# Another hand-written order of steps for a local-attention and SwiGLU kernel on one core

## The chip, the cores and the metric

The kernel runs on one core of a Trainium2 chip. The metric is the device time of one execution in microseconds (us); of several runs the median is given. Engines are named as in the profile: PE (matmuls; PEld its weight loads), DVE, ACT, POOL, and SP, which computes nothing and issues DMAs. "banks" is the accumulator memory that PE writes: eight banks of 128 x 512 float32.

## The reference

Two parts follow each other. First an attention for 4 batches, 8 heads, 768 positions and head size 64, with a bias that falls linearly with distance; a position sees the last 96 positions and the first 8 ("global") keys. Then, on the 4 x 768 = 3072 tokens of 8 x 64 = 512 numbers, a SwiGLU layer with 1536 hidden units. Cut to what matters:

```python
keep = (pos_k < 8) | ((rel >= 0) & (rel < 96))            # rel = query - key
scores = q @ k.T / sqrt(64) - slope[h] * dist              # dist: rel, or 96 for far globals
a = softmax(where(keep, scores, -1e9))
x = (a @ v).transpose(0, 2, 1, 3).reshape(3072, 512)
g, val = x @ w_gate, x @ w_val                             # 512 -> 1536
out = (g * sigmoid(g) * val) @ w_out                       # 1536 -> 512
```

Inputs and output are float32; on the chip the matmuls take float16.

## The kernel before, in words

**Tiling.** A batch has two halves of 384 positions. Batch b and half h make tile t = 2b + h of 384 tokens; eight tiles pass through the second part. The heads of a batch are taken in four pairs (0 to 3), two pairs to a head group.

**What sets the order.** Nothing is scheduled by a program: the string `ORDER` (L67 to L147) lists steps, the last loop of the kernel runs them in this order, and each step records its instructions. Each engine executes its own instructions in that order, one behind the other, and waits at an instruction whose inputs or whose destination are not ready; everything behind it on the same engine waits too. DMAs are issued by the engine that the step names and queue there in the same way: SP issues transposes and output transfers, POOL nearly all loads (L292, L333, L344, L351, L356).

```python
for step in ORDER.split():
    name, *args = step.split(".")
    WORK[name](*(int(a) if a.isdigit() else a for a in args))
```

**Banks.** `single` and `double` deal one or two of the eight banks to a step while the steps are recorded, and `release` puts them back at the end of a list. So the order of the steps also decides which earlier step a matmul must wait for before it may overwrite a bank. In the same way buffers go round: two for output rows (`osb`), two for V (`vS`), two each for the staged rows of keys (`kst`) and queries (`qst`), two for transposed keys (`kN`), four for transposed queries (`qT`).

**The steps that matter here**, with the lines that record them:

- Warm-up: `fill.n` is n matmuls on ones (L394), ahead of the first real work; `fill.23` stands at the end of the order before.
- Batch 0: `Lh` loads half of the keys or queries, `T` transposes them on PE (L417), `cast` changes types (L400) on ACT (`.A`) or DVE (`.V`).
- Batch 1: its first two pairs come by two big loads (`L4`, L333), its other rows by one load per head (`Lr`, L344: a row load; `Lr.b.i.h` has i = 0 for keys and 1 for queries). Batches 2 and 3 come by row loads alone.
- `D.b.p.i` transposes the rows of head pair p (i = 0 keys, 1 queries) by a DMA on SP's queue (L483); `K` copies the keys into place (L490).
- `Z.b.P` is the clearing: POOL writes zeros into two corners of batch b's V buffer (L309), which it may do when the batch that had the buffer before is done with it. `Lv.b.c` then loads chunk c of V, seven chunks per batch (L292). `G` copies the global rows of V on SP (L303). `X` makes the crossed copy of V (L319), which needs all its chunks.
- Attention: `c` scores (L520), `x` exponentials on ACT (L530), `m` masks on DVE, `w` sums for the softmax (L630, L597), `W` weighs V (the L614 matmuls, one block per batch, half and head group), `i`, `j`, `r` (L659, L663) turn the sums into reciprocals and put them in place, `p` scales (L678).
- Second part: `g.t.f` and `v.t.f` are the products of gates and values (L693, four matmuls each: a product step), f being one of twelve blocks of hidden units; `ga` and `gb` (or `va` and `vb`) are its two halves of two matmuls. `t` is a tanh on ACT (L699), `s` and `h` are the rest of the activation on DVE (L703, L709).
- `o.t.i.part` is a fourth of an output row block (L734, three matmuls: an output part; L723 in the last rows), `e.t.i` the output copy of the finished block on ACT into an `osb` buffer (L752) and its transfer by SP (L753; L747 and L748 in the last rows).

While the products of one tile run, the loads, transposes and scores of the next batch are under way; the order mixes their steps by hand.

Of the kernel before, what the change touches and what calls it, by code (L numbers as in the profile page):

```python
# [809 lines left out]
```

## Time and profile before

| | |
|---|---|
| time before | 238.52 us, median of 3 runs (237.11 to 238.77) |
| the profiled execution | 237.59 us |
| its span, first to last instruction | 235.8 us |
| moved by DMA | 25.97 MB, mean 110 GB/s |
| granted clock of PE, mean | 1.000 |

Rows of the views read so. In a group, "PE banks L693 x116" is engine, destination, line and count, with the busy time and the stretch ahead of it. A row of the order in time gives start, duration (or the sum of a run of equal instructions), engine, line, operation, destination<-sources, shape, and in brackets how long the engine stood before it and for what. A row of a window gives start:end, its length, then PE, PEld, DVE, ACT, POOL and SP busy (with counts), the granted clock, the busy share of the DMA engines and GB/s. A row of a waits view gives the waiting instruction, what released it, and the time, count and longest. "SPq" and "POOL ... DMA_DIRECT2D" rows are the issue of a DMA, not its transfer; "DMA to landing" is the time from issue until the data are there.

### The profile page before, as it was taken

The numbers are of one execution on the slowest core, as the hardware profiler recorded it, in microseconds if no ns is written. First come the engines' busy times: TensorE is split into PE (matmuls) and PEld (weight loads), VectorE is DVE, ScalarE is ACT, GpSimd is POOL, SyncE is SP. The second block draws the span as 40 slices with busy tenths as digits, with TensorE's granted clock in tenths as the row PEclk, the third lists the DMA queues.
The fourth block names the chain that finished last, engine by engine and source line by source line (L and its number), as shares of the span: only waits on it lengthen the run. The fifth ranks groups of instructions, "written<-read, shape, count | busy, mean of one in ns | idle before, by whom it ended". The sixth has DMA issues, their size and how long they took to land.

```text
span 235.8 us, 6107 instructions
## 1 busy us (share of the span) xinstructions
PE 229.6 (97%) x2515; PEld 133.6 (57%) x2515; DVE 169.5 (72%) x389; ACT 116.3 (49%) x219; POOL 79.8 (34%) x113
## 2 busy tenths in 40 slices
PE   7999899998999999999999999999999999999998
PEld 4466566554455666655556556565555565555446
DVE  3998898869466789969979998984495876542200
ACT  3688847546842734357858674440424341311321
POOL 8976759731581599788100000000000000000000
DMA  6999999999999899999996311010012000010332
GB/s 171 194 180 188 204 197 178 171 140 122 188 145 184 190 161 135 124 153 153 143 204 152 39 49 47 0 47 0 3 44 89 0 3 0 1 44 3 135 129 93
DMA packets 88324, 25.97 MB, mean 110 GB/s; under 512 B 78048, under 2 KB 85256, under 8 KB 88296
## 3 DMA queue, kind: packets, MB, share of 16 engines
q0 software_dynamic: 67120, 14.25, 79.2%
q1 hardware_dynamic: 20488, 10.74, 23.4%
q10 hardware_dynamic: 688, 0.59, 0.7%
q8 instruction: 19, 0.31, 0.6%
q14 instruction: 9, 0.07, 0.1%
HBM read 28.93 MB, written 6.29 MB: 149 GB/s over the span
## 4 chain that ended last, share of the span: by engine, by line
PE 66%; DMA 23%; POOL 7%; ACT 3%; issue 1%; POOLq 0%; ACTq 0%
PE banks L693 39%; PE banks L734 20%; DMA kst<-in_k_dram 9%; DMA wo<-in_moe_w_out_dram 8%; DMA wv<-in_moe_w_val_dram 4%; DMA out_dram<-osb 2%; POOL vS L292 2%; PE banks L520 2%; PE banks L614 2%; PE banks L723 1%; PE banks L394 1%; POOL k L284 1%; POOL q L284 1%; POOL wg L351 1%; PE banks L630 1%
## 5 line engine op out<-in xcount | busy, mean ns | idle before, releaser
L699 ACT ACTIVATE th<-banks 128x384 f32<-128x384 f32 x96 | 44.3, 494 | 59.4 <-PE banks L693 56.4
L693 PE MATMUL banks<-xT,wv 128*128 128x384 f16 x384 | 71.4, 326 | 0.0
L693 PE MATMUL banks<-xT,wg 128*128 128x384 f16 x384 | 71.2, 326 | 0.1
L709 DVE TENSOR_TENSOR hT<-banks,sl 128x384 f16<-128x384 f32 x96 | 50.8, 552 | 21.2 <-PE banks L693 19.8
L734 PE MATMUL banks<-wo,hT 128*128 128x512 f16 x276 | 65.8, 379 | 0.0
L703 DVE SCALAR_TENSOR_TENSOR sl<-th,banks 128x384 f32<-128x384 f32 x96 | 50.1, 547 | 17.3 <-ACT th L699 16.7
L693 PEld LDWEIGHTS <-wv 128*128 128x128 f16 x384 | 37.3, 98 | 26.3
L693 PEld LDWEIGHTS <-wg 128*128 128x128 f16 x384 | 36.7, 98 | 25.6 <-issue 0.6
L734 PEld LDWEIGHTS <-hT 128*128 128x128 f16 x276 | 26.3, 98 | 28.2 <-issue 0.2
L530 ACT ACTIVATE at<-banks 128x976 f16<-128x976 f32 (+3 forms) x28 | 25.5, 958 | 12.1 <-PE banks L520 12.1
L292 POOL DMA_DIRECT2D vS<-in_v_dram x28 | 25.2, 908 | 9.8 <-DMA vS<-in_v_dram 6.7
L752 ACT ACTIVATE osb<-banks 128x512 f32<-128x512 f32 x23 | 13.5, 599 | 23.3 <-PE banks L734 14.6
L344 POOL DMA_DIRECT2D qst<-in_q_dram x20 | 17.2, 860 | 8.8 <-DMA wo<-in_moe_w_out_dram 4.1
L539 DVE TENSOR_TENSOR at<-at,masks 128x976 f16<-128x976 f16 (+3 forms) x26 | 15.7, 643 | 4.1 <-ACT at L530 4.1
L663 DVE STREAM_TRANSPOSE rb<-dR 128x384 f32<-128x384 f32 x32 | 16.7, 553 | 2.8 <-ACT dR L659 2.7
L344 POOL DMA_DIRECT2D kst<-in_k_dram x20 | 16.7, 841 | 2.6 <-DMA vS<-in_v_dram 1.1
L520 PE MATMUL banks<-qT,kT 64*64 64x152 f16 (+9 forms) x456 | 9.2, 214 | 1.6 <-DMA qT<-qst 1.6
L520 PEld LDWEIGHTS <-kT 64*64 64x64 f16 x456 | 7.2, 107 | 5.8 <-issue 4.8
L678 DVE TENSOR_TENSOR xT<-banks,rb 128x384 f16<-128x384 f32 x16 | 8.4, 546 | 1.3 <-PE banks L614 1.2
L319 ACT COPY vX<-vS 64x1792 f16<-64x1792 f16 (+2 forms) x6 | 7.3, 1220 | 3.3 <-DMA kst<-in_k_dram 3.2
L637 ACT COPY ns<-banks 128x768 f32<-128x768 f32 x6 | 4.7, 807 | 7.9 <-PE banks L614 7.9
L614 PEld LDWEIGHTS <-vS 64*64 64x64 f16 x228 | 6.6, 107 | 2.6 <-issue 2.1
(77 smaller groups left out, 165.2 us busy)
## 6 DMA issues: line engine op xcount, KB each, us to landing
out_dram<-osb SPq DMA_DIRECT2D x23, 256.0 KB, 2.1
vS<-in_v_dram POOLq DMA_DIRECT2D x24, 120.0 KB, 7.7
qst<-in_q_dram POOLq DMA_DIRECT2D x20, 96.0 KB, 7.2
kst<-in_k_dram POOLq DMA_DIRECT2D x20, 96.0 KB, 6.7
wg<-in_moe_w_gate_dram POOLq DMA_DIRECT2D x6, 256.0 KB, 7.3
wv<-in_moe_w_val_dram POOLq DMA_DIRECT2D x6, 256.0 KB, 8.2
wo<-in_moe_w_out_dram POOLq DMA_DIRECT2D x3, 512.0 KB, 18.2
k<-in_k_dram POOLq DMA_DIRECT2D x3, 192.0 KB, 5.7
```

The source lines that it names most:

```text
L292: nc.gpsimd.dma_start(out=v_of(b)[r0:r0 + n, c, heads(g), :], in_=v[b, heads(g), KC * c:KC * c + n, :].rearrange("h p d -> p h d"))
L344: nc.gpsimd.dma_start(out=rows_of(i, b, h // 2)[:, :, h % 2, :], in_=KQ[i][b, h].rearrange("(t p) d -> p t d", p=128))
L520: nc.tensor.matmul(sc[64 * r:64 * r + 64, hi, col:col + n], lhsT=kTs[2 * g + r][d, k0:k0 + 64], rhs=qTs[b, 2 * g + r][d, q0:q0 + n], start ...
L530: nc.scalar.activation(out=at[:, :, 0:w], in_=sc[:, :, 0:w], func=AF.Exp, scale=scale)
L539: ENG[e].tensor_mul(a2, a2, masks[:, 2 * g:2 * g + 2, x:x + w])
L663: nc.vector.transpose(rb.rearrange("p (n i) -> p n i", i=32), rbs[b, half][:, g, r].unsqueeze(2).broadcast_to([128, TB // 32, 32]))
L693: nc.tensor.matmul(gv[t, f, which][:, 0:TB], lhsT=w[:, c, 128 * f:128 * f + 128], rhs=xTs[t][:, c, :], start=(c == 0), stop=(c == NC - 1))
L699: nc.scalar.activation(out=th, in_=gv[t, f, 0][:, 0:TB], func=AF.Tanh, scale=0.5)
L703: nc.vector.scalar_tensor_tensor(out=sl, in0=gv[t, f, "t"], scalar=1.0, in1=gv[t, f, 0][:, 0:TB], op0=AluOp.add, op1=AluOp.mult)
L709: nc.vector.tensor_mul(hTs[t][:, f, :], gv[t, f, 1][:, 0:TB], gv[t, f, "s"])
L734: nc.tensor.matmul(ops_t[t, i], lhsT=hTs[t][:, f, 128 * i:128 * i + 128], rhs=wo[:, f, :], start=(f == 0), stop=(f == NFF - 1))
L752: nc.scalar.mul(out=osb, in_=ops, mul=0.5)
```

## The change

Only the string `ORDER` is changed. Every step but these stays as it was and stands elsewhere: `fill.11 fill.5` (16 warm-up matmuls) become `fill.24`, and `fill.23` at the end is dropped; `g.0.1`, `v.0.8`, `v.0.9` and `v.0.10` are split into their halves; three casts, some copies of transposed keys and queries, crossed copies of V and copies of reciprocals change between ACT and DVE; some of batch 1's and batch 3's weighted values are no longer copied out by ACT first (`n`). The last weighted block of batch 1's first half, `W.1.1.0`, moves behind eleven product steps of tile 2.

**ACT** (th: a tanh; at: an exponential; osb: an output copy; vX<-vS: the crossed copy of batch 1's V; dR: reciprocals). Around the crossed copy, before:

```order
L530 ACTIVATE at<-banks 128x1008
L530 ACTIVATE at<-banks 128x2x488
L319 COPY vX<-vS 64x1792
L659 COPY dR<-dR 32x24 x4
L752 ACTIVATE osb<-banks 128x512 x3
L659 COPY dR<-dR 32x24 x4
L752 ACTIVATE osb<-banks 128x512
L699 ACTIVATE th<-banks 128x384
L637 COPY ns<-banks 128x768
```

and now:

```order
L530 ACTIVATE at<-banks 128x2x480
L530 ACTIVATE at<-banks 128x1008
L319 COPY vX<-vS 64x1792
L752 ACTIVATE osb<-banks 128x512
L659 COPY dR<-dR 32x24 x4
L752 ACTIVATE osb<-banks 128x512 x2
L699 ACTIVATE th<-banks 128x384
L752 ACTIVATE osb<-banks 128x512 x2
L699 ACTIVATE th<-banks 128x384 x17
```

The first output copy (`e.1.2`) stands directly behind the crossed copy, five output copies follow within two groups of others, and the two copies of weighted values (ns, L637) are gone from here. The bank of the first copy goes to `o.0.0.0`, those of the next four to `v.2.2`, `g.2.6`, `v.2.3` and `g.2.8`.

**POOL**, the first clearing of a V buffer that was in use (kst, qst with 6x64: row loads; wg, wv: weights). Before, where kst_605 and qst_603 are batch 1's rows and vS_936 is batch 2's V, in the buffer of batch 0:

```order
L351 DMA wg_78<-in_moe_w_gate_dram 128x2x512
L344 DMA kst_605<-in_k_dram 128x6x64 x2
L309 MEMSET vS_936 32x256
L309 MEMSET vS_936 128x256
L351 DMA wv_79<-in_moe_w_val_dram 128x2x512 x2
```

and now, where kst_633 and qst_635 are batch 1's rows and vS_803 is batch 3's V, in the buffer of batch 0:

```order
L344 DMA kst_633<-in_k_dram 128x6x64 x2
L351 DMA wg_78<-in_moe_w_gate_dram 128x2x512
L309 MEMSET vS_803 32x256
L309 MEMSET vS_803 128x256
L344 DMA kst_633<-in_k_dram 128x6x64
L344 DMA qst_635<-in_q_dram 128x6x64 x2
L351 DMA wg_78<-in_moe_w_gate_dram 128x2x512
```

The clearing stood behind all row loads of batch 1; now five of them (three here, two more behind the weights) stand behind it, and it is batch 3 that gets this buffer.

**POOL**, the second clearing. Before, where kst_968 and qst_1122 are batch 2's rows, kst_1626 and qst_1628 batch 3's, vS_936 batch 2's V and vS_1605 batch 3's, in the buffer of batch 1:

```order
L344 DMA qst_1122<-in_q_dram 128x6x64
L344 DMA kst_968<-in_k_dram 128x6x64
L309 MEMSET vS_1605 32x256
L309 MEMSET vS_1605 128x256
L344 DMA kst_1626<-in_k_dram 128x6x64
L344 DMA qst_1628<-in_q_dram 128x6x64
L292 DMA vS_936<-in_v_dram 120x8x64
```

and now, where kst_919 and qst_1257 are batch 2's rows, vS_1675 is batch 2's V, in the buffer of batch 1, and vS_803 batch 3's:

```order
L344 DMA kst_919<-in_k_dram 128x6x64
L344 DMA qst_1257<-in_q_dram 128x6x64 x2
L309 MEMSET vS_1675 32x256
L309 MEMSET vS_1675 128x256
L292 DMA vS_1675<-in_v_dram 48x8x64
L292 DMA vS_803<-in_v_dram 48x8x64
L344 DMA kst_919<-in_k_dram 128x6x64
L292 DMA vS_1675<-in_v_dram 120x8x64 x3
```

In both orders it waits for batch 1's weighted values; before, it was the buffer of batch 3 that waited, now it is that of batch 2, and all chunks of V of both batches stand behind it.

**SP** (kN: keys transposed, qT: queries transposed, out<-osb: outputs). Before:

```order
L303 DMA vS_87<-vS_87 8x3x512
L483 DMA_TRANSPOSE kN_841<-kst_605 128x6x128
L483 DMA_TRANSPOSE qT_889<-qst_603 128x6x128
L483 DMA_TRANSPOSE kN_932<-kst_605 128x6x128
L483 DMA_TRANSPOSE qT_934<-qst_603 128x6x128
L303 DMA vS_115<-vS_115 8x6x512
L483 DMA_TRANSPOSE kN_1231<-kst_968 128x6x128
L753 DMA out_0_dram<-osb_1387 128x512
L753 DMA out_0_dram<-osb_1427 128x512
L483 DMA_TRANSPOSE qT_1430<-qst_1122 128x6x128
```

and now:

```order
L303 DMA vS_86<-vS_86 8x3x512
L483 DMA_TRANSPOSE kN_729<-kst_633 128x6x128
L483 DMA_TRANSPOSE qT_866<-qst_635 128x6x128
L483 DMA_TRANSPOSE kN_868<-kst_633 128x6x128
L483 DMA_TRANSPOSE qT_881<-qst_635 128x6x128
L303 DMA vS_118<-vS_118 8x6x512
L753 DMA out_0_dram<-osb_1386 128x512
L483 DMA_TRANSPOSE kN_1528<-kst_919 128x6x128
L753 DMA out_0_dram<-osb_1539 128x512
L753 DMA out_0_dram<-osb_1542 128x512
L483 DMA_TRANSPOSE kN_1555<-kst_919 128x6x128
```

The four transposes of batch 1 stand in the same sequence of kinds, though of the pairs 2, 3, 3, 2 (before 3, 2, 2, 3); behind them the first output transfer now stands ahead of the first transpose of batch 2.

The diff, cut to lines that hold these pieces:

```diff
-Lf.A.1.1 Z.0.P pre Lf.S.0.1 Lf.A.1.0 cast.1.1.V Li cast.1.0.V fill.11 fill.5 Z.1.P kz.P sl.1 sl.7
...
-x.0.1.1.0 x.0.1.1.1 Lw.0.2.1 g.0.1 Lw.1.2.0 t.0.1 g.0.2 g.0.3 t.0.3 Lw.1.2.1 t.0.2 m.0.0.1.1.V w.0.1
...
-t.0.11 s.0.11 p.0.1.1.1.V Lw.0.1.0 v.0.10 h.0.9 h.0.11 U.1.1 U.0.1 U.0.0 U.1.0 qw.1.A t.0.10 D.1.3.0
...
-g.1.1 Lr.1.0.5 t.1.11 g.1.9 g.1.6 D.1.2.0 D.1.3.1 Z.2.P Lw.1.1.1 t.1.1 s.1.11 h.1.10 s.1.3 t.1.6
...
-o.1.0.2 i.1.0 j.1.0.A o.1.2.1 o.0.2.1 i.1.1 Lr.2.0.2 Lr.2.1.4 r.1.1.0.0 Lr.2.0.1 e.0.0 o.1.0.3
-o.1.2.2 o.1.2.3 W.1.0.0 e.1.0 D.2.3.1 D.2.2.1 W.1.0.1 r.1.0.0.1 o.0.1.1 o.0.1.2 p.1.0.0.1.V
-p.1.1.0.0.V o.0.1.3 r.1.1.0.1 e.1.2 j.1.1.A r.1.0.0.0 p.1.1.0.1.V p.1.0.0.0.V o.0.2.2 o.0.2.3 g.2.3
-e.0.2 t.2.3 D.2.3.0 W.1.1.0 W.1.1.1 n.1.0.1 r.1.1.1.1 r.1.0.1.0 g.2.4 g.2.6 r.1.0.1.1 g.2.7 t.2.4
-v.2.6 Z.3.P s.2.3 s.2.4 n.1.1.1 g.2.1 g.2.2 t.2.6 t.2.2 Lr.3.0.6 Lr.3.1.6 p.1.0.1.1.V v.2.3 v.2.4
...
-fill.23 e.7.0 e.7.3 e.7.2
+Z.0.P pre Lf.A.1.1 fill.24 Z.1.P Lf.S.0.1 Lf.A.1.0 cast.1.1.A cast.0.1.V cast.1.0.A Li kz.P sl.1
...
+p.0.1.1.1.V W.0.1.0 r.0.0.1.0 t.0.11 t.0.9 U.0.0 s.0.9 Z.3.P h.0.10 p.0.0.1.0.V U.1.0 v.0.11
+p.0.0.1.1.V g.1.10 Lr.1.0.7 s.0.11 Lr.1.1.6 Lr.1.1.7 U.1.1 U.0.1 kw.1.A h.0.9 Lw.0.1.1 qw.1.A
+D.1.3.1 D.1.3.0 h.0.11 Lr.1.1.5 Lr.1.1.4 g.1.3 g.1.0 D.1.2.1 Lw.1.1.1 kw.0.V v.1.0 qw.0.A t.1.3
...
+o.0.2.1 Lr.2.0.2 o.0.1.0 o.1.2.2 m.1.0.1.1.V m.1.1.0.0.V o.1.2.3 Lr.2.0.0 Lr.2.0.4 X.1.1.0.7.A w.1.1
+i.1.1 w.1.0 o.0.1.1 i.1.0 o.1.0.2 o.0.2.2 o.0.2.3 X.1.0.0.7.V Lr.2.1.5 Lr.2.1.7 e.1.2 j.1.0.V
+Lr.2.0.6 r.1.1.0.0 Lr.2.1.3 o.0.1.2 o.0.0.0 W.1.0.1 r.1.0.0.1 W.1.0.0 o.1.0.3 Lr.2.1.6 Lr.2.1.0
...
+o.0.1.3 r.1.1.0.1 W.1.1.1 D.2.3.0 p.1.1.0.1.V Lr.2.1.4 r.1.1.1.1 g.2.4 e.0.2 e.1.0 g.2.6 t.2.4
+r.1.1.1.0 s.2.4 D.2.2.0 D.2.0.1 p.1.1.1.1.V v.2.2 v.2.6 r.1.0.1.0 g.2.3 e.0.1 D.2.1.1 p.1.1.1.0.V
+e.0.0 v.2.3 t.2.6 g.2.8 D.2.2.1 g.2.9 s.2.6 g.2.1 t.2.3 t.2.1 g.2.2 r.1.0.1.1 h.2.6 s.2.3 t.2.9
+h.2.3 s.2.1 v.2.4 W.1.1.0 t.2.8 g.2.10 h.2.4 g.2.5 Z.2.P t.2.2 s.2.8 p.1.0.1.1.V p.1.0.1.0.V Lv.2.6
...
+o.7.0.2 o.7.0.3 o.7.2.0 o.7.2.1 o.7.2.2 o.7.2.3 e.7.1 e.7.0 e.7.3 e.7.2
```

136 lines of the change are left out of this document (67 added, 69 removed).

## The prediction

> **What bounds the kernel now.** I read the profile in this order: the page's busy times, the stages by window, who waited for whom on PE, then PE, SP, ACT and POOL in order of time around each wait.
>
> ```profile
> span 235.8 us, 6107 instructions
> PE 229.6 (97%) x2515; PEld 133.6 (57%) x2515; DVE 169.5 (72%) x389; ACT 116.3 (49%) x219; POOL 79.8 (34%) x113
> 57.61:79.78 22.17, 20.22 (x345) 10.91 (x345) 13.70 (x30) 11.95 (x22) 9.74 (x13) 1.00 1.78 182
> 79.78:232.32 152.54, 152.54 (x1446) 86.66 (x1446) 108.57 (x239) 66.61 (x126) 29.39 (x34) 1.00 0.74 75
> 79.78 19.01 PE banks L693 x116
> ```
>
> PE is the bound. From 79.78 to 232.32 it is busy in all 152.54 us, at full granted clock (the 1.00); from 57.61 to 79.78 it is idle for 22.17 - 20.22 = 1.95. A product matmul passes in 19.01 / 116 = 0.164 us, so a step of four takes 0.65. Both programs hold the same matmuls but for the warm-up, so an order can win only what PE waits now and lose only by new waits. The waits:
>
> ```profile
> PE banks L520 <- DMA qT<-qst: 1.6, 1, 1.6
> PE banks L630 <- issue: 0.8, 1, 0.8
> PE banks L614 <- ACT osb L752: 0.3, 1, 0.3
> 57.61 0.26 PE L520 MATMUL banks<-qT,kT 64*64 64x160 f16 x2
> 59.43 0.81 PE L520 MATMUL banks<-qT,kT 64*64 64x160 f16 x42 [1.56 <-DMA qT<-qst]
> 71.85 0.25 PE L614 MATMUL banks<-at,vS 64*64 64x152 f16 x2
> 76.03 0.81 PE L693 MATMUL banks<-xT,wg 128*128 128x384 f16 x4
> 77.20 0.24 PE L614 MATMUL banks<-at,vS 64*64 64x128 f16 x2 [0.35 <-ACT osb L752]
> 78.27 2.33 PE L693 MATMUL banks<-xT,wg 128*128 128x384 f16 x12
> 80.43 0.81 PE L693 MATMUL banks<-xT,wv 128*128 128x384 f16 x4
> ```
>
> The reader is to see two places. At 57.61 PE begins batch 1's scores of the second head group and stands 1.56 us until the last transposed queries land: I call this **the wall**. Around 77 it loses 77.20 - 76.03 - 0.65 = 0.52 and, in twelve products that fill 80.43 - 78.27 = 2.16 instead of 1.95, another 0.21: together 0.73, because ACT hands no banks back.
>
> **The change, part by part.**
>
> *Start to the wall.* The wall is a chain of four transposes on SP's queue:
>
> ```profile
> 35.93 1.34 SPq L483 DMA_TRANSPOSE kN<-kst  x1
> 39.73 1.35 SPq L483 DMA_TRANSPOSE qT<-qst  x1
> 43.42 1.27 SPq L483 DMA_TRANSPOSE kN<-kst  x1
> 44.87 4.38 SPq L483 DMA_TRANSPOSE qT<-qst  x1
> DMA to landing us min/median/max: 6.9/6.9/6.9
> DMA to landing us min/median/max: 8.5/11.5/14.5
> ```
>
> The first landing row is that of the keys (the first of them, 35.93 + 6.9 = 42.8), the second that of the queries: 39.73 + 8.5 = 48.2 and 44.87 + 14.5 = 59.4. From 42.8 to 59.4 three land in 16.6 us, 5.5 each, although the last was issued early enough: they are served one behind the other, and the chain ends at its start plus four services. It starts with the first pair of key rows, the third load behind the two big ones of batch 1 in both programs, so I keep 35.9.
>
> In the new order PE has the same work ahead of this place (all gates and values of tiles 0 and 1, three score pieces). What it gains before is swallowed by the wait, and a loss is covered up to 1.56 us. That takes in the halved gates and values, the two half-1 loads now ahead of V's first chunk, the casts that change between ACT and DVE, and the 0.8 that the sums of tile 0 stand for "issue". The largest loss is the warm-up:
>
> ```profile
> 1.19 3.60 PE L394 MATMUL banks<-ones 128*128 128x256 f16 x16 [1.19 <-DVE ones L362]
> 4.83 0.53 PE L417 MATMUL banks<-ident,q 128*64 128x128 f16 x6
> 232.15 2.67 PE L394 MATMUL banks<-ones 128*128 128x256 f16 x23
> ```
>
> 16 matmuls take 3.60 (0.225 each); 24 take 5.4 and end at 6.6, so the first transposes slip from 4.83 by at most 1.8, and by 0.9 if the extra eight ran at the pace of the last row (2.67 / 23 = 0.116). Either is about the cover. The Trainium skill ("TensorE: Matmul & The Clock Gate", Part 1) says that the slow clock ends after some 3.4 us of sustained work, whatever the number of matmuls, in a window that runs free. The rows show 16 slow ones over 3.60 us; by that rule the 24 would end near 5.7 instead of 6.6, and the sum is the same.
>
> What can push the chain itself is POOL's first clearing of a V buffer. It now stands ahead of the rows that the second transpose needs, and waits until batch 0's V has been used, the L614 matmuls of tile 1. Those move behind seven more product steps:
>
> ```profile
> 28.69 0.20 PE L614 MATMUL banks<-at,vS 64*64 64x72 f16 x2
> DMA to landing us min/median/max: 6.7/9.1/9.5
> ```
>
> 28.9 + 7 x 0.65 = 33.4; clearing to 34.1; the third row load behind it is issued at 35.8 and lands 6.7 to 9.5 later (batch 1's key loads), 42.5 to 45.3, while the chain wants it at 42.8. POOL's pause leaves less in the queue ahead of it, so I take a value near the low end, +0.3; bounds -1.5 (the wall falls with its wait) and +2.5.
>
> *Wall to batch 1's weighted values.* Both orders put five score pieces, two sums and fifteen output parts between the wall and the first L614 matmul of batch 1: 71.85 - 59.43 = 12.42 us. New is where the bank of the last of these parts (tile 0, rows 0) comes from: from ACT's first output copy, which now stands directly behind the copy that waits for batch 1's V.
>
> ```profile
> 68.25 1.69 ACT L319 COPY vX<-vS 64x1792 f16<-64x1792 f16 x1 [3.23 <-DMA kst<-in_k_dram]
> 70.86 1.09 ACT L752 ACTIVATE osb<-banks 128x512 f32<-128x512 f32 x2
> 76.55 0.60 ACT L752 ACTIVATE osb<-banks 128x512 f32<-128x512 f32 x1 [4.60 <-DMA out_dram<-osb]
> DMA to landing us min/median/max: 3.3/4.4/5.0
> ```
>
> The V copy begins at 68.25 now, when V has landed. One more row load stands ahead of V's last chunk, 0 to the 0.83 of one issue (79.84 below): 0.4. Then 68.65 + 1.69 + 0.60 = 70.9. PE wants the bank at 59.43 + 12.42 - 0.65 = 71.2. The two meet: 0, up to +1.5 if V lands later. If the wall should fall alone, this is the next wait, and it takes the gain back.
>
> *ACT's output copies.* Now ACT sits 4.60 us because its third copy needs one of two buffers whose transfer has not landed (3.3 to 5.0 us for the five of this stretch, the last row above). The 0.73 around 77 follows from that. In the new order five copies follow each other with one tanh between, through the same two buffers. At the median of 4.4 the first ends at 71.0, the third starts at 75.4 and ends at 76.0, and the fifth ends at 80.4 + 0.6 = 81.0. PE wants the fifth's bank at 71.85 + 11 steps of 0.65 + three L614 blocks of 0.5 (two of them fill 77.20 to 78.27) = 80.5. At 3.3 there is no wait, at 4.4 one of 0.5, at 5.0 one of 1.7. I take 0.4, a little under the median, since no transpose is issued just ahead of the first transfer. Term -0.73 + 0.4 = -0.3; bounds -0.7 and +1.0.
>
> *POOL's second clearing.* Batch 3's V is set up before batch 2's, so batch 2 takes batch 1's buffer, and its clearing stands on POOL ahead of all of batch 2's V. It waits until PE's last use of batch 1's V, which moves behind eleven product steps.
>
> ```profile
> 78.54 0.68 POOL L309 MEMSET vS<- 32x256 uint32 x2 [6.78 <-ACT dR L659]
> 79.84 0.83 POOL L344 DMA_DIRECT2D kst<-in_k_dram  x1 [0.62 <-issue]
> 98.49 0.84 POOL L344 DMA_DIRECT2D qst<-in_q_dram  x1 [0.88 <-DMA qst<-in_q_dram]
> DMA to landing us min/median/max: 5.2/7.5/9.0
> DMA to landing us min/median/max: 10.0/16.1/17.7
> ```
>
> Now the clearing starts at 78.54, 0.3 behind the L614 block. Then the block ends at 71.85 + 16 steps of 0.65 + four blocks of 0.5 = 84.2, and the clearing starts at 84.5. V's last chunk is the 21st load behind it; the 21st now is issued at 98.49, 19.95 behind, so then at 104.4, and lands 5.2 to 9.0 later (V's loads from 79 to 113). Behind it on ACT stand V's copy (1.69), a tanh and an output copy, 2.9 together, whose bank PE wants 56 steps and some 320 small matmuls behind 71.85: 36.4 + 5.0, with the 0.4 above, 113.7. At a median of 7.5 the bank is free at 114.8, 1.1 late; at 5.2 in time; at 9.0 2.6 late. I take 0.9; bounds 0 and +2.6.
>
> *Rest and end.* From 84 on PE has no wait now, and the new order's bank re-uses are no closer, so 0. The closing 23 matmuls go; SP's exit waits for them:
>
> ```profile
> SPq L805 <- PE banks L394: 0.6, 1, 0.6
> 232.67 0.33 SPq L748 DMA_DIRECT2D out_dram<-osb  x1
> ```
>
> They end at 232.15 + 2.67 = 234.82. The last output is issued at 232.67 and may be over sooner; SP names 0.6 for the matmuls. I take 0.5; bounds 0 and 0.6.
>
> **Sum**: +0.3 + 0 - 0.3 + 0.9 + 0 - 0.5 = +0.4 on the profiled execution's 237.59 us (span 235.8 and 1.8 around it), which is 0.9 below the median of the three runs, 238.52. In the terms of that median: 238.9.
>
> **Rivals.**
>
> *The walls fall.* If the transposes are slow only because they share the DMA engines with POOL's loads, and POOL now pauses at its first clearing, the chain and V's last chunk come sooner. For it:
>
> ```profile
> DMA to landing us min/median/max: 2.8/5.5/14.5
> ```
>
> These are all twenty transposes: the quiet ones 2.8, the last of batch 1 14.5. Against it: the pause costs load time that V needs. Price: -1.5 at the wall, -0.7 at the output copies, -0.5 at the end, no new wait: 235.8. The Trainium skill ("DMA: Bandwidth & Descriptors", Queues, rings and completion order) says that a DMA engine takes turns between the queues that have work, packet by packet. By that rule a pause of one queue speeds the other, which speaks for this rival; the 2.8 against 14.5 agrees with it. Chance 0.18.
>
> *V of batch 2 decides.* V's loads are as slow as batch 1's were beside their transposes (the last row of POOL's fence, V's loads from 40 to 70 us, 10.0 to 17.7). It decides from a landing at 110.8 on. At 10.0 V lands at 114.4, the bank is free at 117.3, 3.6 late instead of 0.9: 241.6; at the median 16.1 it would be 247.7. For it: V's loads, the next rows and the last transposes of batch 2 now fall together. Against it: the 5.2 to 9.0 of that stage now. Chance 0.23.
>
> *The chain starts its second service late.* The rows behind the first clearing take the median of 9.1: 44.9, 2.1 late instead of 0.3: 240.7. Against it: the queue is emptier then. Chance 0.09.
>
> **How the numbers follow.** The forecast has 0.50; its own range is 237.3 to 240.4 (the terms at half their bounds). A measurement of this kernel tells about 1% (2.4 us) from no change. Faster by more needs the first rival, 0.18; slower by more the second and a little of the third, 0.25; the rest is 0.57. The range of 8 in 10 reaches to the first two rivals: 235.8 to 241.6.
>
> **What would show it.** Right: PE stands before batch 1's second score group until 59 to 60; batch 1's L614 matmuls begin at 71.5 to 72.5; the fifth output copy ends near 81; POOL's second clearing starts near 84; ACT's V copy of batch 2 ends near 114 after a wait for a DMA; no closing matmuls, and a tail 0.5 shorter. Wrong: PE passing the wall without standing, an L614 start before 70, a second clearing that delays nothing, or a stand of PE above 1 us behind 115.

## The result, and the profile after

The changed kernel takes 240.56 us (median of 4 runs, 240.25 to 241.66) against 238.0 (4 runs): a ratio of 1.0124, 95% interval 1.0085 to 1.0163. Slower, then, by a little over the 1% that the prediction took as the least that can be told from no change. The time lies in the prediction's widest range (235.8 to 241.6) and just above the forecast's own (237.3 to 240.4); the likeliest case was 238.9, and the sum of +0.4 stands against a measured +2.6. The profiled execution of the changed kernel took 241.66, the longest of the four. Its page begins:

```profile
span 239.9 us, 6083 instructions
PE 230.8 (96%) x2500; PEld 132.8 (55%) x2500; DVE 167.0 (70%) x393; ACT 119.0 (50%) x212; POOL 79.5 (33%) x113
PEclk9999999999599999999999999999999999999999
```

The eleventh slice shows a halved clock. PE in order of time, and by window (behind the length PE's busy time; third from the end the granted clock, last GB/s):

```profile
59.61 0.67 PE L520 MATMUL banks<-qT,kT 64*64 64x128 f16 x32 [1.98 <-DMA qT<-qst]
60.97 2.74 PE L734 MATMUL banks<-wo,hT 128*128 128x512 f16 x6 [0.69 <-DMA wo<-in_moe_w_out_dram]
...
57.00:58.00 1.00, 0.63 (x4) 0.28 (x3) 1.00 (x5) 0.00 (x0) 0.64 (x1) 1.00 2.47 145
58.00:59.00 1.00, 0.00 (x0) 0.00 (x0) 1.00 (x3) 0.00 (x0) 0.00 (x0) 1.00 1.49 167
59.00:60.00 1.00, 0.39 (x29) 0.39 (x31) 1.00 (x3) 0.00 (x0) 0.18 (x1) 1.00 1.29 205
60.00:61.00 1.00, 0.31 (x19) 0.10 (x7) 0.77 (x2) 0.90 (x2) 0.74 (x1) 0.52 1.43 195
65.00:66.00 1.00, 1.00 (x11) 0.42 (x4) 0.00 (x0) 1.00 (x2) 0.75 (x1) 0.50 2.22 164
66.00:67.00 1.00, 1.00 (x4) 0.32 (x3) 0.00 (x0) 1.00 (x2) 0.09 (x1) 0.56 3.62 128
```

PE stands 1.98 for the transposed queries (1.56 before), then 0.69 for output weights, and from 60.0 to 66.9 its clock is halved (0.52 in the first of these windows, 0.50, then 0.56). That stretch hides what else is late there, so the same kernel was profiled once more (`a_again`). At full clock the order on PE reads:

```profile
58.08 0.62 PE L520 MATMUL banks<-qT,kT 64*64 64x128 f16 x32
59.38 1.47 PE L734 MATMUL banks<-wo,hT 128*128 128x512 f16 x6 [0.68 <-DMA wo<-in_moe_w_out_dram]
64.14 2.53 PE L734 MATMUL banks<-wo,hT 128*128 128x512 f16 x11 [2.20 <-DMA wo<-in_moe_w_out_dram]
73.09 0.81 PE L734 MATMUL banks<-wo,hT 128*128 128x512 f16 x3 [0.15 <-ACT osb L752]
83.61 0.81 PE L693 MATMUL banks<-xT,wv 128*128 128x384 f16 x4 [1.49 <-ACT osb L752]
```

Here the stand before batch 1's scores is gone, and two others have come: 0.68 + 2.20 = 2.9 us for the first two chunks of the output weights, which no step of the prediction names, and 1.49 for the bank of the fourth output copy. The rows of ACT and SP behind the second one:

```profile
70.73 1.68 ACT L319 COPY vX<-vS 64x1792 f16<-64x1792 f16 x1 [6.46 <-DMA vS<-in_v_dram]
72.44 0.60 ACT L752 ACTIVATE osb<-banks 128x512 f32<-128x512 f32 x1
77.34 0.60 ACT L752 ACTIVATE osb<-banks 128x512 f32<-128x512 f32 x1 [2.79 <-DMA out_dram<-osb]
82.96 1.24 ACT L752 ACTIVATE osb<-banks 128x512 f32<-128x512 f32 x2 [2.92 <-DMA out_dram<-osb]
```

```profile
73.06 0.35 SPq L753 DMA_DIRECT2D out_dram<-osb  x1
75.41 1.22 SPq L483 DMA_TRANSPOSE kN<-kst  x1
76.73 1.56 SPq L753 DMA_DIRECT2D out_dram<-osb  x2
78.46 1.25 SPq L483 DMA_TRANSPOSE kN<-kst  x1
79.81 2.09 SPq L483 DMA_TRANSPOSE qT<-qst  x1
```

The second output copy ends at about 74.6, but its transfer is issued at 76.73: SP stood from 73.41 (the end of its issue at 73.06) to 75.41 at a transpose whose rows had not landed and then needed 1.22 for its issue. ACT's fourth copy, which needs that buffer, waits 2.92 us and starts at 82.96.

To add such losses up I give each step on PE a lag: its start, less the matmul work ahead of it at the usual pace of each kind (0.65 us for a product step). Where the lag grows, PE lost time. Its growth in five stretches, less that in the trace of before, worked out from all PE rows of each trace (another choice of the usual pace moves an entry by up to 0.2):

| trace | to batch 1's second group of scores | to its first L614 matmul | to 90 us | to the last output part | tail | sum |
|---|---|---|---|---|---|---|
| changed, first trace | +0.3 | +3.4 | +0.5 | +0.3 | -0.4 | +4.1 |
| changed, full clock (`a_again`) | -1.2 | +3.2 | +1.7 | +0.3 | -0.4 | +3.5 |
| `a_clear_late` | -1.8 | +0.2 | +1.6 | +0.2 | -0.4 | -0.1 |
| `a_wo_early` | -0.1 | +0.6 | +1.7 | +0.2 | -0.4 | +2.0 |
| `a_clear_outs` | -1.8 | +0.3 | 0.0 | +0.3 | -0.4 | -1.6 |
| `a_best` | -1.2 | -0.2 | -0.1 | +1.8 | -0.4 | -0.2 |
| `a_best_v2` | -1.4 | -0.2 | -0.2 | +0.3 | -0.4 | -1.9 |
| `b_no_fill` | -0.9 | -0.1 | -0.5 | 0.0 | -0.4 | -2.0 |

The first column moves by 1.5 us between executions of one kernel, so the sums of single traces are not verdicts.

### The profile page after: what moved, and what is told of

Its sections match the earlier page's. It is cut to its first block, busy times and chain, and to the rows that moved or that the text cites. A ratio compares the mean times of both kernels' runs of the same rounds, so it can differ in the third digit from the quotient of the medians.

```text
span 239.9 us, 6083 instructions
## 1 busy us (share of the span) xinstructions
PE 230.8 (96%) x2500; PEld 132.8 (55%) x2500; DVE 167.0 (70%) x393; ACT 119.0 (50%) x212; POOL 79.5 (33%) x113
## 4 chain that ended last, share of the span: by engine, by line
PE 66%; DMA 21%; POOL 5%; issue 3%; ACT 2%; DVE 1%; POOLq 0%; ACTq 0%; DVEq 0%
PE banks L693 40%; PE banks L734 20%; DMA vS<-in_v_dram 7%; DMA wo<-in_moe_w_out_dram 7%; DMA out_dram<-osb 4%; DMA wg<-in_moe_w_gate_dram 3%; PE banks L520 2%; PE banks L614 2%; PE banks L630 1%; POOL vS L292 1%; PE banks L723 1%; POOL k L284 1%; POOL q L284 1%; POOL vS L309 1%; ACT vX L319 1%
## 5 line engine op out<-in xcount | busy, mean ns | idle before, releaser
L734 PE MATMUL banks<-wo,hT 128*128 128x512 f16 x276 | 68.3, 389 | 0.7 <-DMA wo<-in_moe_w_out_dram 0.7
L530 ACT ACTIVATE at<-banks 128x1008 f16<-128x1008 f32 (+3 forms) x28 | 25.4, 955 | 15.6 <-PE banks L520 15.3
L539 DVE TENSOR_TENSOR at<-at,masks 128x1008 f16<-128x1008 f16 (+3 forms) x26 | 15.8, 644 | 7.9 <-ACT at L530 7.8
L663 DVE STREAM_TRANSPOSE rb<-dR 128x384 f32<-128x384 f32 x32 | 17.4, 561 | 0.1
L319 ACT COPY vX<-vS 64x1792 f16<-64x1792 f16 (+2 forms) x9 | 11.2, 1256 | 4.2 <-DMA vS<-in_v_dram 4.1
L678 DVE TENSOR_TENSOR xT<-banks,rb 128x384 f16<-128x384 f32 x22 | 11.3, 545 | 0.8 <-issue 0.7
L520 PEld LDWEIGHTS <-kT 64*64 64x64 f16 x456 | 7.8, 113 | 7.2 <-issue 6.6
L520 PE MATMUL banks<-qT,kT 64*64 64x152 f16 (+9 forms) x456 | 9.8, 224 | 2.0 <-DMA qT<-qst 2.0
L614 PEld LDWEIGHTS <-vS 64*64 64x64 f16 x228 | 6.7, 107 | 3.0 <-issue 2.5
L309 POOL MEMSET vS<- 32x256 uint32 (+1 forms) x8 | 2.5, 309 | 16.7 <-ACT th L699 12.4
```

The costliest lines, as they stand in the source:

```text
L520: nc.tensor.matmul(sc[64 * r:64 * r + 64, hi, col:col + n], lhsT=kTs[2 * g + r][d, k0:k0 + 64], rhs=qTs[b, 2 * g + r][d, q0:q0 + n], start ...
L530: nc.scalar.activation(out=at[:, :, 0:w], in_=sc[:, :, 0:w], func=AF.Exp, scale=scale)
L539: ENG[e].tensor_mul(a2, a2, masks[:, 2 * g:2 * g + 2, x:x + w])
L663: nc.vector.transpose(rb.rearrange("p (n i) -> p n i", i=32), rbs[b, half][:, g, r].unsqueeze(2).broadcast_to([128, TB // 32, 32]))
L734: nc.tensor.matmul(ops_t[t, i], lhsT=hTs[t][:, f, 128 * i:128 * i + 128], rhs=wo[:, f, :], start=(f == 0), stop=(f == NFF - 1))
```

## The experiments

All times are medians; each ratio is against runs of the kernel before on the same chip (237.7 for the first two sets of four, 237.6 for the next three, 238.3 for the last).

**The changed kernel again, `a_again`.** No edit.

> The changed kernel once more, for a trace at full clock. The first one showed PE at a granted clock of 0.50 from 60.0 to 66.6 us, and V's last chunk of batch 1 landing at 71.6 instead of 68.1. The bank theory: the time to batch 1's weighted values is set by V's last chunk (71.6), its crossed copy (1.7) and the output copy behind it (0.6), so at full clock PE stands there some 2.5 us for a bank, and the time stays at 240.3 to 240.8, 1% over before. The clock theory: the loss of that trace is the slow clock, 3.3 us in 6.6; at full clock 237.5 to 238.5 and no stand.

Measured: 240.54 us, ratio 1.011 (1.0067 to 1.0152), the trace above, clock 1.00. The clock theory falls: at full clock nothing is won. Of ten runs of the changed kernel five had a mean clock of 1.00 and took 240.1 on average (median 240.4), five had 0.986 or 0.993 and took 240.8 (median 240.6). The bank theory named the right stretch and the wrong wait: the bank costs 0.15, since the output weights have already held PE up.

**The first output copy ahead of V's copy, `a_copy_first`.**

```diff
-o.0.2.1 Lr.2.0.2 o.0.1.0 o.1.2.2 m.1.0.1.1.V m.1.1.0.0.V o.1.2.3 Lr.2.0.0 Lr.2.0.4 X.1.1.0.7.A w.1.1
-i.1.1 w.1.0 o.0.1.1 i.1.0 o.1.0.2 o.0.2.2 o.0.2.3 X.1.0.0.7.V Lr.2.1.5 Lr.2.1.7 e.1.2 j.1.0.V
+o.0.2.1 Lr.2.0.2 o.0.1.0 o.1.2.2 m.1.0.1.1.V m.1.1.0.0.V o.1.2.3 Lr.2.0.0 Lr.2.0.4 e.1.2 X.1.1.0.7.A w.1.1
+i.1.1 w.1.0 o.0.1.1 i.1.0 o.1.0.2 o.0.2.2 o.0.2.3 X.1.0.0.7.V Lr.2.1.5 Lr.2.1.7 j.1.0.V
```

> The changed kernel with one step moved: the first output copy stands ahead of the crossed copy of V on ACT, so that its bank no longer waits for V. The bank theory: PE passes the last output part at about 71 and then stands for the crossed copy itself, to 73.3; the L614 matmuls start 1.3 us earlier than in the changed kernel (the output copy's 0.6 and the output part's 0.65 behind it go), time -1.3. The clock theory: no change.

Measured: 241.05, 1.0113 (1.0066 to 1.0161): no gain. Who PE waited for:

```profile
PE banks L734 <- DMA wo<-in_moe_w_out_dram: 2.6, 2, 1.6
PE banks L630 <- DVE dT L647: 0.8, 1, 0.8
PE banks L630 <- ACT osb L752: 0.7, 1, 0.7
```

The wait for the output weights is there, untouched. Since banks are dealt in the order of the steps, the earlier copy also gave its bank to the softmax sums (L630), which now wait for it. As a test of the bank this says little; it shows that the order of release is part of such a move.

**POOL's first clearing behind the row loads, `a_clear_late`.**

```diff
-p.0.1.1.1.V W.0.1.0 r.0.0.1.0 t.0.11 t.0.9 U.0.0 s.0.9 Z.3.P h.0.10 p.0.0.1.0.V U.1.0 v.0.11
+p.0.1.1.1.V W.0.1.0 r.0.0.1.0 t.0.11 t.0.9 U.0.0 s.0.9 h.0.10 p.0.0.1.0.V U.1.0 v.0.11
...
-D.1.3.1 D.1.3.0 h.0.11 Lr.1.1.5 Lr.1.1.4 g.1.3 g.1.0 D.1.2.1 Lw.1.1.1 kw.0.V v.1.0 qw.0.A t.1.3
+D.1.3.1 D.1.3.0 h.0.11 Lr.1.1.5 Lr.1.1.4 Z.3.P g.1.3 g.1.0 D.1.2.1 Lw.1.1.1 kw.0.V v.1.0 qw.0.A t.1.3
```

> The changed kernel with POOL's first clearing behind all row loads of batch 1, so that no load waits for it. If the clearing's pause makes V late: the row loads behind it are issued up to 3.7 us earlier, the chain of transposes ends before 59, V's last chunk lands at 69.5 to 70, time -1.5. If V is late for the loads ahead of it in the queue alone: the chain up to 1 us earlier, V at 71 to 71.6, time within 0.5.

Measured: 237.82, 1.0011 (0.9987 to 1.0035). This one step is worth 2.7 us, as much as the whole loss; the interval lies clear of that of `a_again`. It is more than either expectation, and V's last chunk lands at 67.2, earlier than the 69.5 that was expected. The time of before is reached by a balance, not for want of losses: in the table +1.6 at the output copies stands against -1.8 and -0.4. POOL at the clearing and at the output weights, with these loads' time to landing, first in `a_again`, then here:

```profile
34.08 0.67 POOL L309 MEMSET vS<- 32x256 uint32 x2 [3.81 <-issue]
45.86 1.64 POOL L356 DMA_DIRECT2D wo<-in_moe_w_out_dram  x2
64.38 0.83 POOL L344 DMA_DIRECT2D kst<-in_k_dram  x1 [2.99 <-DMA wo<-in_moe_w_out_dram]
DMA to landing us min/median/max: 18.2/19.0/19.7
```

```profile
37.38 0.68 POOL L309 MEMSET vS<- 32x256 uint32 x2
44.26 1.55 POOL L356 DMA_DIRECT2D wo<-in_moe_w_out_dram  x2 [0.48 <-DMA qst<-in_q_dram]
DMA to landing us min/median/max: 15.4/16.1/16.8
```

The second chunk of weights lands at 45.86 + 18.2 = 64.1 with the clearing's stand of 3.81 ahead of the row loads, and at 44.26 + 15.4 = 59.7 without. (In the trace of before it lands at 44.29 + 18.2 = 62.5, just as PE comes to read it.) 4.4 us come of 1.6 in the issue. What goes with it: the stretch in which transposes and loads are under way together ends sooner. Windows of before, of `a_again` and of `a_clear_late` (the last number is GB/s):

```profile
53.00:58.00 5.00, 4.87 (x48) 2.71 (x47) 4.92 (x13) 3.87 (x7) 0.90 (x1) 1.00 1.85 111
58.00:65.00 7.00, 5.57 (x97) 3.02 (x97) 3.71 (x8) 5.17 (x6) 3.34 (x4) 1.00 1.60 187
```

```profile
53.00:58.00 5.00, 5.00 (x49) 2.99 (x48) 4.46 (x15) 3.06 (x5) 0.64 (x1) 1.00 2.22 111
58.00:65.00 7.00, 4.12 (x92) 2.19 (x92) 5.05 (x11) 4.49 (x5) 3.28 (x4) 1.00 1.44 199
```

```profile
53.00:58.00 5.00, 5.00 (x60) 3.00 (x58) 4.61 (x14) 3.06 (x5) 2.67 (x3) 1.00 1.43 198
58.00:65.00 7.00, 7.00 (x95) 3.30 (x87) 5.65 (x11) 4.49 (x5) 2.63 (x4) 1.00 1.90 177
```

From 53 to 58 only 111 GB/s pass in `a_again` while transposes are under way, and 198 in `a_clear_late`, where the last packets of the four transposes pass before 53 (58 in `a_again`). That the transposes are what holds the loads down there is argued from this, not shown by a run of its own. PE is then busy in all 7.00 us of the stretch behind, instead of 4.12.

**Matmuls on ones in the stand, `a_fill_wall`.**

```diff
-t.1.5 K.1.3 s.1.5 v.1.4 v.1.5 h.0.7 h.1.4 c.1.1.1.0 Lv.1.3 x.1.1.1.0 h.1.5 c.1.1.0.1 o.1.2.0 o.1.0.0
+t.1.5 K.1.3 s.1.5 v.1.4 v.1.5 h.0.7 h.1.4 fill.16 c.1.1.1.0 Lv.1.3 x.1.1.1.0 h.1.5 c.1.1.0.1 o.1.2.0 o.1.0.0
...
-        warm = single("f") if spare else banks[:, 7, :]
+        warm = banks[:, freed[0] if spare else 7, :]
...
-        if spare:
-            release("f")
```

> The changed kernel with 16 matmuls on ones (1.9 us at full clock) where PE stands for the last transposed queries, in a bank that is free there. The clock theory: the stand of 2 us is what brings the slow clock; the granted clock stays 1.00 in every run, time -1 to -3 where the runs of the changed kernel show less than 1.00. The bank theory: the clock may stay up, but PE then stands for the bank of the first output copy, and the time stays within 0.7 of the changed kernel.

Measured: 239.52, 1.0069 (1.0033 to 1.0104). The clock was 0.999 or 1.00 in 11 of 12 runs, against 5 of 10 without the fill, which speaks for the stand bringing the halved clock. The time fell by 1.0, which the intervals don't separate from the changed kernel's. That a halved clock costs so little here (240.6 against 240.4 in the medians above) fits a stretch in which PE would stand for late data anyway: with the fill and at full clock, PE still waits 1.5 us for output weights in the trace of `a_fill_wall`.

**The output transfers ahead of four transposes, `a_outs_first`.**

```diff
-o.0.1.3 r.1.1.0.1 W.1.1.1 D.2.3.0 p.1.1.0.1.V Lr.2.1.4 r.1.1.1.1 g.2.4 e.0.2 e.1.0 g.2.6 t.2.4
-r.1.1.1.0 s.2.4 D.2.2.0 D.2.0.1 p.1.1.1.1.V v.2.2 v.2.6 r.1.0.1.0 g.2.3 e.0.1 D.2.1.1 p.1.1.1.0.V
-e.0.0 v.2.3 t.2.6 g.2.8 D.2.2.1 g.2.9 s.2.6 g.2.1 t.2.3 t.2.1 g.2.2 r.1.0.1.1 h.2.6 s.2.3 t.2.9
+o.0.1.3 r.1.1.0.1 W.1.1.1 p.1.1.0.1.V Lr.2.1.4 r.1.1.1.1 g.2.4 e.0.2 e.1.0 g.2.6 t.2.4
+r.1.1.1.0 s.2.4 p.1.1.1.1.V v.2.2 v.2.6 r.1.0.1.0 g.2.3 e.0.1 p.1.1.1.0.V
+e.0.0 D.2.3.0 D.2.2.0 D.2.0.1 D.2.1.1 v.2.3 t.2.6 g.2.8 D.2.2.1 g.2.9 s.2.6 g.2.1 t.2.3 t.2.1 g.2.2 r.1.0.1.1 h.2.6 s.2.3 t.2.9
```

> The changed kernel with four transposes of batch 2 moved on SP's queue behind the five output transfers that they stood between. In the trace of the changed kernel at full clock PE loses 1.65 us at the fourth output copy's bank and 0.4 two steps on; the second output copy's transfer was issued 2.2 us after its copy ended, behind a transpose that waited for its rows, and landed 6 us after that. If that queue is the cause: the stand at that bank goes, time -1.4 to -2.0 against the changed kernel, 238.5 to 239.1. If ACT's two buffers alone set it, or the transposes are then missed: within 0.5.

Measured: 239.08, 1.0031 (0.9993 to 1.0068), 1.5 less than the changed kernel, as expected of SP's queue, though the interval touches that of `a_again`. Its profiled execution was 2 us longer than its median, so only the place is read from it: the fourth copy starts without a wait, the fifth after one of 1.89; PE's stand of 1.49 at the fourth copy's bank is gone, and 0.30 is left at the fifth's.

```profile
80.34 0.59 ACT L752 ACTIVATE osb<-banks 128x512 f32<-128x512 f32 x1
82.82 0.60 ACT L752 ACTIVATE osb<-banks 128x512 f32<-128x512 f32 x1 [1.89 <-DMA out_dram<-osb]
...
83.47 1.79 PE L693 MATMUL banks<-xT,wg 128*128 128x384 f16 x10 [0.30 <-ACT osb L752]
```

**Both repairs, `a_clear_outs`.** The edits of `a_clear_late` and `a_outs_first` together.

> Both repairs together: the changed kernel with POOL's first clearing behind all row loads of batch 1, and with the five output transfers ahead of the four transposes on SP. If the two losses are separate: 2.7 and 1.4 to 2.0 less than the changed kernel, 235.8 to 236.4, faster than before by 0.6 to 0.8%. If one hides in the other: 237 to 238.

Measured: 236.74, 0.9958 (0.9932 to 0.9985), faster than before, with an interval below that of `a_clear_late`. The gains are 2.7 and 1.1: separate, the second a little under its range. No stand over 0.3 us is left between 57 and 90. The product step that waits for the fourth output copy's bank, in `a_clear_late` and here (both at full clock):

```profile
80.05 0.81 PE L693 MATMUL banks<-xT,wv 128*128 128x384 f16 x4 [1.42 <-ACT osb L752]
```

```profile
78.49 0.81 PE L693 MATMUL banks<-xT,wv 128*128 128x384 f16 x4
```

The move does two things that no run separates: the second output transfer is issued as soon as its copy ends, instead of 2.2 us later, and it is faster, 4.9 us from issue to landing (3.8 in `a_outs_first`) where in `a_again` some 6 pass before ACT may use its buffer again.

**Output weights ahead of V, `a_wo_early`.**

```diff
-t.1.0 h.0.8 Lw.1.1.0 g.1.8 g.1.11 g.1.2 g.1.9 s.1.3 s.1.0 Lr.2.0.7 Lv.1.4 M.2.0 M.0.0 v.1.3 t.1.8
-s.1.8 h.1.0 v.1.9 Lv.1.0 v.1.10 v.1.11 t.1.10 t.1.9 s.1.10 t.1.11 t.1.2 h.1.3 Lo.0 Lv.1.1 s.1.9
-v.1.8 s.1.11 s.1.2 h.1.11 h.1.9 c.1.0.0.1 c.1.0.0.0 g.1.7 g.1.6 x.1.0.0.0 h.1.10 x.1.0.0.1 Lo.1
+t.1.0 h.0.8 Lw.1.1.0 Lo.0 Lo.1 g.1.8 g.1.11 g.1.2 g.1.9 s.1.3 s.1.0 Lr.2.0.7 Lv.1.4 M.2.0 M.0.0 v.1.3 t.1.8
+s.1.8 h.1.0 v.1.9 Lv.1.0 v.1.10 v.1.11 t.1.10 t.1.9 s.1.10 t.1.11 t.1.2 h.1.3 Lv.1.1 s.1.9
+v.1.8 s.1.11 s.1.2 h.1.11 h.1.9 c.1.0.0.1 c.1.0.0.0 g.1.7 g.1.6 x.1.0.0.0 h.1.10 x.1.0.0.1
```

> The changed kernel with the first two chunks of output weights ahead of batch 2's first row load and of V on POOL. In the trace at full clock PE stands 0.7 and 2.2 us for these two chunks before the L614 matmuls of batch 1, and 0.3 for a bank that waits for V. If the weights are the cause alone: both stands go, time -2.5. If V's lateness stands behind them: V's last chunk lands where it did (70.7), PE stands some 3 us for the bank of the first output copy instead, and the time stays within 0.7.

Measured: 238.96, 1.0032 (1.0003 to 1.0061), 1.6 less than the changed kernel: between the two expectations. PE's waits:

```profile
PE banks L520 <- DMA qT<-qst: 1.6, 1, 1.6
PE banks L693 <- ACT osb L752: 1.5, 1, 1.5
PE banks L734 <- ACT osb L752: 0.7, 1, 0.7
```

The weights are no longer waited for; 0.7 for the bank behind V and 1.6 for the queries stand in their place. So the weights were the wait that ended last in that stretch, with others close behind.

**The kernel before without its closing matmuls, `b_no_fill`.**

```diff
-fill.23 e.7.0 e.7.3 e.7.2
+e.7.0 e.7.3 e.7.2
```

> The kernel before without its 23 closing matmuls on ones. The forecast had them at 0.5 us, between 0 and 0.6: time -0.4 to -0.5, and the tail from the last output product to the end of the span 2.6 us instead of 3.0. If the last output's transfer sets the end anyway: no difference.

Measured: 237.09, 0.9957 (0.9926 to 0.9988), -0.6; the tail is 0.4 shorter (2.6 instead of 3.0), in this and in every kernel of the table, all of which lack the closing matmuls.

**Batch 2's first row loads behind V, `a_rows_late`.** `Lr.2.0.7` and `Lr.2.0.5` stand directly behind `Lv.1.5`.

```diff
-t.1.0 h.0.8 Lw.1.1.0 g.1.8 g.1.11 g.1.2 g.1.9 s.1.3 s.1.0 Lr.2.0.7 Lv.1.4 M.2.0 M.0.0 v.1.3 t.1.8
+t.1.0 h.0.8 Lw.1.1.0 g.1.8 g.1.11 g.1.2 g.1.9 s.1.3 s.1.0 Lv.1.4 M.2.0 M.0.0 v.1.3 t.1.8
...
-m.1.0.1.0.V m.1.0.0.0.V c.1.1.1.1 Lv.1.5 c.1.0.1.1 x.1.1.0.1 m.1.0.0.1.V c.1.1.0.0 Lr.2.1.2
+m.1.0.1.0.V m.1.0.0.0.V c.1.1.1.1 Lv.1.5 Lr.2.0.7 Lr.2.0.5 c.1.0.1.1 x.1.1.0.1 m.1.0.0.1.V c.1.1.0.0 Lr.2.1.2
```

> The changed kernel with batch 2's first two row loads moved behind the last chunk of batch 1's V on POOL; the first clearing stays ahead of the row loads of batch 1. In the trace of the changed kernel at full clock the first of them took 3.5 us of the queue (its landing 51.0 behind 47.6), ahead of V and the output weights. If the place in the queue is what makes these late: the second chunk of output weights lands 2 to 3.5 us earlier (64.1 before), the stands for weights and bank go, time -2 to -3. If the transposes that run beside the loads set the pace, whichever loads those are: landings earlier by one row load alone (0.6 to 1.3), time -0.5 to -1.3.

Measured: 241.86, 1.0156 (1.0111 to 1.0201). Neither: no gain, and possibly a loss. In its trace (an execution 1.2 us above the median) PE stands for the queries instead:

```profile
PE banks L520 <- DMA qT<-qst: 3.0, 1, 3.0
```

One load less ahead of the weights bought nothing while the transposes ran beside V's loads: the second chunk is issued at 45.33 instead of 45.86 and lands at 65.2 instead of 64.1. The place in POOL's queue alone does not set these landings.

**The output transfers first in the kernel before, `b_outs_first`.** Without `fill.23`, and `D.2.2.0 D.2.3.1 D.2.2.1` directly behind `e.0.2`.

```diff
-o.1.0.0 Lr.2.1.5 c.1.0.1.1 D.2.2.0 m.1.0.0.0.V c.1.1.1.0 x.1.1.1.1 M.3.0 Lr.2.1.7 Lr.2.0.6 o.0.0.1
+o.1.0.0 Lr.2.1.5 c.1.0.1.1 m.1.0.0.0.V c.1.1.1.0 x.1.1.1.1 M.3.0 Lr.2.1.7 Lr.2.0.6 o.0.0.1
...
-o.1.2.2 o.1.2.3 W.1.0.0 e.1.0 D.2.3.1 D.2.2.1 W.1.0.1 r.1.0.0.1 o.0.1.1 o.0.1.2 p.1.0.0.1.V
+o.1.2.2 o.1.2.3 W.1.0.0 e.1.0 W.1.0.1 r.1.0.0.1 o.0.1.1 o.0.1.2 p.1.0.0.1.V
...
-e.0.2 t.2.3 D.2.3.0 W.1.1.0 W.1.1.1 n.1.0.1 r.1.1.1.1 r.1.0.1.0 g.2.4 g.2.6 r.1.0.1.1 g.2.7 t.2.4
+e.0.2 D.2.2.0 D.2.3.1 D.2.2.1 t.2.3 D.2.3.0 W.1.1.0 W.1.1.1 n.1.0.1 r.1.1.1.1 r.1.0.1.0 g.2.4 g.2.6 r.1.0.1.1 g.2.7 t.2.4
```

> The kernel before, without the closing matmuls, and with its first four output transfers ahead of three transposes on SP. Without the closing matmuls alone it took 237.1. If SP's queue sets the 0.7 that PE loses around 77 us there: 236.4. If ACT's two buffers alone do: 237.1.

Measured: 238.78, 1.005 (1.0018 to 1.0082), 1.7 more than `b_no_fill`. The 0.7 around 77 us is gone, but that says little, since in the trace of `b_no_fill` only some 0.2 of it is left without the move. What is new is a wait of batch 2's scores:

```profile
110.24 0.60 PE L520 MATMUL banks<-qT,kT 64*64 64x152 f16 x28 [1.98 <-DMA qT<-qst]
```

The queries that they wait for are not among the three that were moved: their transpose stands further back in the same queue and is issued at 102.72 (98.27 in `b_no_fill`). That the move delayed it is argued from the queue; part of the difference arose ahead of the edit, at the wall. The time shows that what was free to move in the changed order was not free in the order before.

**All repairs, `a_best`, and with V's last chunk early, `a_best_v2`.** The edits of `a_clear_outs` and `a_rows_late`, and `v.2.4` behind `W.1.1.0`; the second kernel also moves `Lv.2.4` directly behind `Lv.2.1`.

```diff
-h.2.3 s.2.1 v.2.4 W.1.1.0 t.2.8 g.2.10 h.2.4 g.2.5 Z.2.P t.2.2 s.2.8 p.1.0.1.1.V p.1.0.1.0.V Lv.2.6
+h.2.3 s.2.1 W.1.1.0 v.2.4 t.2.8 g.2.10 h.2.4 g.2.5 Z.2.P t.2.2 s.2.8 p.1.0.1.1.V p.1.0.1.0.V Lv.2.6
...
-s.2.10 Lv.2.5 t.3.1 Lr.3.0.6 s.2.11 s.3.1 t.2.0 Lv.2.3 v.3.1 v.2.11 h.3.8 Lv.3.4 g.3.0 Lv.2.1 s.2.0
+s.2.10 Lv.2.5 t.3.1 Lr.3.0.6 s.2.11 s.3.1 t.2.0 Lv.2.3 v.3.1 v.2.11 h.3.8 Lv.3.4 g.3.0 Lv.2.1 Lv.2.4 s.2.0
```

> The changed kernel with all repairs: the first clearing behind the row loads of batch 1, the output transfers ahead of four transposes, batch 2's first two row loads behind V, and one product step of tile 2 (whose bank came from the product's use two steps earlier) behind the last L614 block. The trace with the first two repairs still had 0.4 us at the first output copy's bank and 0.4 at that product step. If both go: 235.9, against 236.7 with two repairs; 0.8% faster than before. If a wait takes their place: 236.5 to 237.

> The version with all repairs, and V's last chunk of batch 2 moved from the 21st to the 11th load behind POOL's second clearing. In the trace of the version with all repairs this chunk landed at 111.8, ACT stood 2.25 us for it before the crossed copy, and PE 1.4 us for the bank of the output copy behind; in the changed kernel, where everything was 3.6 us later there, the same chunk came just in time. If that is the forecast's fourth term at work: PE's stand before the gate and value products of tile 3 goes, time -0.5 to -1.2 (it shows only in part of the runs), 235.0 to 235.6. If the chunk only changes places with another wait: 236.1.

Measured: 236.14, 0.9939 (0.991 to 0.9967), between its two expectations and not to be told from `a_clear_outs`; and 235.67, 0.9899 (0.9858 to 0.994). The second is faster than both kernels. The crossed copy of batch 2's V on ACT, and PE behind it, in the changed kernel (first trace), in `a_clear_outs`, in `a_best` and in `a_best_v2`:

```profile
115.56 1.68 ACT L319 COPY vX<-vS 64x1792 f16<-64x1792 f16 x1
```

```profile
110.40 1.69 ACT L319 COPY vX<-vS 64x1792 f16<-64x1792 f16 x1 [0.56 <-issue]
```

```profile
111.92 1.68 ACT L319 COPY vX<-vS 64x1792 f16<-64x1792 f16 x1 [2.25 <-DMA qst<-in_q_dram]
...
114.65 0.81 PE L693 MATMUL banks<-xT,wv 128*128 128x384 f16 x4 [1.41 <-ACT osb L752]
```

```profile
109.60 1.68 ACT L319 COPY vX<-vS 64x1792 f16<-64x1792 f16 x1
```

In the changed kernel and in `a_clear_outs` V's last chunk comes just in time (it lands at 115.2 and 110.3), although everything ahead was 4.2 us late in the one and 1.6 early in the other (the first three columns of the table). In `a_best` it lands at 111.8 and PE stands 1.41 us. The lateness does not decide it, since POOL's second clearing moves with PE: it starts at 89.45, 83.79 and 82.77. What differs is the time from the clearing to the chunk's landing: 25.8 and 26.5 us, and 29.0 in `a_best`. Why it is longer there stays open. Moving the chunk takes the stand away in the trace of `a_best_v2`. The two intervals overlap, so the 0.5 between the medians rests on the traces.

## Why the prediction was right or wrong

That the time lies in the widest range is in part luck: the upper end of that range was set by a rival that did not come, and the larger part of the loss came from a wait that no term names. The forecast's own range is narrower than its working: the terms at half their bounds add up to 237.1 to 242.3, not to 237.3 to 240.4.

**Start to the wall (+0.3): near in its number, not borne out in its chain, and too narrow in what it followed.** The clearing was forecast for 33.4 and begins at 34.08 in `a_again`, behind a stand of 3.81. The third row load behind it was to land at 42.5 or later; the second transpose, which needs it, is issued at 41.72 (39.73 before). It lands at 50.7, and at 52.1 in the first trace, 2.4 and 3.8 later than before (48.3). A chain of equal services would end that much later too. But the wall ended at 59.6 in the first trace, 0.2 later than before, and there was none in the second, where PE began these scores at 58.08. So four equal services do not describe the chain. (The first row below is of `a_again`, the second of the first trace.) The warm-up was bounded by an end at 6.6; the last of the 24 starts at 5.8 and PE's next work at 5.97 (5.54 in `a_again`). That is nearer to 5.7, the prediction's estimate by the rule of the Trainium skill ("TensorE: Matmul & The Clock Gate", Part 1).

```profile
41.72 1.29 SPq L483 DMA_TRANSPOSE qT<-qst  x1
```

```profile
L394 PE MATMUL banks<-ones x24: 272/418/418, 1.2 to 5.8; 128*128 128x256 f16 x24
```

**Wall to batch 1's weighted values (0, up to +1.5): the step that failed.** It followed the clearing's pause into the chain of transposes and not into the rest of POOL's queue. It counted PE's fifteen output parts there as work without asking what they read: the output weights, loaded by that queue and landing just then. PE stood 2.9 us for them in `a_again`. Of that trace's +3.2 in this stretch 1.2 is what the stretch before had won; the prediction foresaw such a giving back, but for the bank behind V. V's last chunk was put 0.4 later and was 2.6 later (70.7 instead of 68.1), which the weights' wait hides. `a_clear_late` shows the place, `a_wo_early` the wait.

**ACT's output copies (-0.3): wrong sign.** The copies were costed through the first, third and fifth of them, at the transfers' median of 4.4, and a little less, "since no transpose is issued just ahead of the first transfer". The loss came through the second and fourth: a transpose stands ahead of the second transfer, waiting for its rows. Measured +1.7 in the lag in `a_again`, 1.49 of it at one bank, and +0.5 in the first trace, where PE came later. The place of the transposes on SP's queue is the cause (`a_outs_first`, and `a_clear_outs` against `a_clear_late`).

**POOL's second clearing (+0.9): the mechanism is there, and cost nothing in the changed kernel's traces.** The sum puts 27.4 us (19.95 + 7.5) between the clearing and the landing of V's last chunk. It was 25.8 in the first trace and 26.4 in `a_again`, and PE did not stand; it was 29.0 in `a_best`, and PE stood 1.4. The clearing itself came 4 to 5 us later than forecast (88.89 and 89.45 instead of 84.5), and PE's need of the bank moved with it.

**End (-0.5): right.** -0.4 by the tail, -0.6 by `b_no_fill`.

**The rivals.** "The walls fall" came half true in the second trace (-1.2 in the first column), and its "no new wait" did not. "The chain starts its second service late" (240.7) named the right clearing, and the second transposed queries did land 2.4 to 3.8 later, but the wall did not follow; the loss came from another load behind the same clearing. "V of batch 2 decides" (241.6) lies nearest to some runs and was not the cause.

## What to carry to other kernels

A pause on a queue delays everything behind it: list each load that comes later in that queue, and ask who reads it first, not only the load that the wait was found at. A wait that a forecast finds costs nothing while a larger one stands ahead, and comes back when that one is mended (the bank behind V: 0.15 in `a_again`, 0.67 in `a_wo_early`). Transfers that free a small pair of buffers should not queue behind a transpose that waits for its own rows, unless the transpose has no slack itself.
